# Hash attention and mixture of adapters: the last third of the attention as one group, and another order of the tail

## The chip, the core and the metric

The kernel runs on one core of one Trainium2 chip. TensorE (PE) does the matrix products, VectorE (DVE), ScalarE (ACT) and GpSimd (POOL) work beside it, and SyncE (SP) issues most of the transfers. The metric is the device time of one execution in microseconds. The profile is that of one execution; its span runs from the first to the last instruction on the core.

## The reference

There are 4 batches of 8 heads, 768 positions, head dimension 64. Each query and key gets a 6-bit bucket from the signs of its product with `proj`; a query attends to the keys of its own bucket:

```python
mask = q_bucket[:, :, :, None] == k_bucket[:, :, None, :]
scores = np.where(mask, scale * np.matmul(q, k.transpose(0, 1, 3, 2)), -1e9)
attn = np.exp(scores - np.max(scores, axis=-1, keepdims=True))
attn = attn / (np.sum(attn, axis=-1, keepdims=True) + 1e-09)
x = np.matmul(attn, v)                 # heads side by side: (B*S, H*D) = (3072, 512)
logits = x @ w_gate                    # 8 experts, the two largest are taken
w = softmax of the two logits
out = x + sum over the two experts e of w_e * ((x @ A[e]) @ B[e])   # rank 16
```

## The kernel before

**Attention.** The heads are taken in 16 pairs, four to a batch. `score` makes a tile of 1024 columns of the transposed scores in PSUM (PE, L328), and ACT turns it into weights with one exponential (L330), nine tiles for a pair. PE multiplies the weights by V, which has a column of ones for the sum (L335, and L407, L435 at the end); DVE takes the reciprocal of the sum and scales. A position index is split into 6 *slots* of 128; a slot is the unit of the second half of the kernel.

**Mixture of adapters.** It needs all 512 features of a position, so it follows a batch's last pair. For a group of slots: `xtrans` or `xtrans2` transposes the bf16 copy `xb` of x on PE and copies it to `xT`; `lgz` multiplies `xT`, in four parts of 128 features (t = 0 to 3, one for each pair of heads), by the router and the first adapter matrix side by side (`wa`) into the tile `lz` (L501); `route_a` finds the largest logits (DVE, L510, L512), `route_e` takes an exponential (ACT, L522), `route_b` makes the gate weights `gw` and the gated `zm` (DVE, L532, L534); `totals` makes the reciprocal `rt` of their sum (L545, L547); `zmtrans` transposes `zm` on PE (L555) and copies it to `zmT` (L558, DVE or ACT); `delta` multiplies by the second matrix (L571) and adds x. The addition is either one DVE instruction (L580), or, with `by_pool`, an ACT scaling (L577) and a POOL addition (L578). Each slot's output, 256 KB, then goes out by a DMA (L583).

**The end.** The order of all work is written out by hand: every engine executes its instructions in the order in which the program emits them, and a waiting instruction holds back those behind it on its engine. The last two pairs (p = 14, q = 15) are handled by `last_two` (L706), in *thirds*: third u is the slots 2u and 2u+1. Its loop runs m = 0 to 17, three steps for each of (p,0), (p,1), (q,0), (q,1), (p,2), (q,2); each step makes one score tile, and the product with V follows with `third` in three parts of eight matmuls after one matmul with `eps` that opens the tile. `third_out` writes x in float32 and has POOL cast it to `xb`; with `fast` (the thirds (q,1) and (p,2)) DVE writes `xb` itself first and x after it. The third (q,2) is different: `pieces` cuts its scores by slot into eight matmuls of 128 columns, and `sixth` handles slot 4 and then slot 5, each in its own PSUM tile with 12 matmuls; `sixth_x` writes `xb` and x, both on DVE. Below, t[0], t[1], t[2] are the groups of slots (0,1), (2,3), (4,5) of the last batch.

After the loop (L778 to L804) the program emits the rest: the second half of `sixth(4)`, the deltas of t[0], the transposes and `lgz` of t[2], then route, transposition and delta of t[1] and t[2]. The deltas of t[0] and t[1] go by ACT and POOL, those of t[2] by DVE. Outputs leave by SP's queue, but for the last ones: one and a half by ACT's queue for t[2], and slot 3 by ACT's queue as the very last instruction (L802).

**PSUM.** Eight banks: the pool `ps_s` has two tiles of two banks, `ps_v` two of one bank, `ps_t` and `ps_m` one each. A tile of a pool can be written when all readers of the tile that was there before are done, so `bank=` in a call also says whom it waits for.

Of the kernel before, what the change touches and what calls it, by code (L numbers as in the profile page):

```python
# [19 lines left out]
class Emitter:  # L20
# [266 lines left out]
    def pieces(self, p, s):  # L287
        S, out = self.S, []
        if p == self.n_pairs - 1 and s >= 6:
            for j in range(8):  # L290
                e, hk = divmod((s - 6) * 8 + j, 2 * self.T)
                h, kt = divmod(hk, self.T)
                i = 3 * e + 2
                out.append((h, kt, self.aug[p % 2][0:71, 2 * h, i * self.P:(i + 1) * self.P], 128, 128 * j))
            return out
        if p >= self.n_pairs - 2:
            for j in range(4):
                h, kt = divmod((s % 3) * 4 + j, self.T)
                q = self.aug[p % 2][0:71, 2 * h, :].rearrange("p (e c) -> p e c", e=2)
                u = s // 3  # L300
                out.append((h, kt, q[:, :, u * self.P:(u + 1) * self.P], 256, 256 * j))
            return out
        at, end = s * 1024, (s + 1) * 1024
        while at < end:
            kt, q0 = divmod(at, S)
            h, kt = divmod(kt, self.T)
            n = min(512 - at % 512, S - q0)
            out.append((h, kt, self.aug[p % 2][0:71, 2 * h, q0:q0 + n], n, at - s * 1024))
            at += n
        return out  # L310

    def p_at(self, p, h, kt, i):
        if p == self.n_pairs - 1 and i % 3 == 2:
            o = 6144 + (i // 3) * 1536 + (h * self.T + kt) * 128
        elif p >= self.n_pairs - 2:
# [98 lines left out]
    def third_out(self, p, u, fast=False):  # L414
        b, hp, sl = self.B - 1, p % self.PPB, slice(2 * u, 2 * u + 2)
        x, xb = self.x[b][:, :, hp * self.P:(hp + 1) * self.P], self.xb[b][:, hp]
        if fast:
            self.third_x(p, u, xb)
        self.third_x(p, u, x)
        if not fast:  # L420
            self.nc.gpsimd.tensor_copy(out=xb[:, sl, :], in_=x[:, sl, :])


    def sixth(self, sl, j0, j1):
        nc, P, T, D = self.nc, self.P, self.T, self.D
        p, b = self.n_pairs - 1, self.B - 1
        if j0 == 0:
            pv = self.ps_v.tile([P, 2, D + 1], F32, tag="v", name=f"pvs{sl}")
            ri = self.smallp.tile([P, 2], F32, tag="ri", name=f"ris{sl}")
            self.pvl[sl] = pv, ri  # L430
            nc.tensor.matmul(out=pv, lhsT=self.eps, rhs=self.vb[p % 3][:, :, T, :], start=True, stop=False)
        pv, ri = self.pvl[sl]
        for j in range(j0, j1):
            h, kt = divmod(j, T)
            nc.tensor.matmul(out=pv[:, h, :], lhsT=self.p_at(p, h, kt, 3 * (sl - 4) + 2),  # L435
                             rhs=self.vb[p % 3][:, h, self.slot(kt), :], start=False, stop=(j == 2 * T - 1))
        if j1 == 2 * T:
            nc.vector.reciprocal(out=ri, in_=pv[:, :, D])
            self.sixth_x(sl, self.xb[b][:, self.PPB - 1])

    def sixth_x(self, sl, dst):
        D = self.D
        pv, ri = self.pvl[sl]
        self.nc.vector.tensor_tensor(
            out=dst[:, sl, :].rearrange("p (h d) -> p h d", h=2), in0=pv[:, :, 0:D],
            in1=ri.unsqueeze(2).to_broadcast([self.P, 2, D]), op=ALU.mult)
# [43 lines left out]
    def lgz(self, b, slots, which=None, bank=None):  # L490
        nc, P = self.nc, self.P
        n = len(slots)
        if which is None or 0 in which:
# [3 lines left out]
        for i, s in enumerate(slots):  # L497
            if which is not None and i not in which:
                continue
            for t in range(self.nD):  # L500
                nc.tensor.matmul(out=lz[:, i, :], lhsT=self.xT[b][:, t, s * P:(s + 1) * P],  # L501
                                 rhs=self.wa[:, t, :], start=(t == 0), stop=(t == self.nD - 1))
# [203 lines left out]
    def last_two(self, p, q, b):  # L706
# [5 lines left out]
        for m in range(18):  # L712
# [34 lines left out]
            for at, k in ((3, 0), (6, 1), (8, 2), (11, 3), (14, 4)):  # L747
                if 0 <= m - at < 3:
                    self.third(*order[k], m - at)
                if m - at == 2:  # L750
                    self.third_out(*order[k], fast=k > 2)
# [16 lines left out]
            if m == 15:  # L768
                self.xtrans2(p, q, t[1], one)
                self.route_e(b, t[0])  # L770
                self.route_b(b, t[0])
            if m == 16:
                self.lgz(b, t[1], bank=far)
                self.route_a(b, t[1], now=False)
            if m == 17:
                self.zmtrans(b, t[0])
                self.sixth(4, 0, 8)
        self.sixth(4, 8, T2)  # L778
        self.sixth_x(4, x)
        self.route_e(b, t[1])  # L780
        self.delta(b, t[0], 0, bank=mid, by_pool=True)
        self.xtrans(p, t[2], on_act=True, bank=free)
        self.sixth(5, 0, 4)
        self.sixth(5, 4, T2)
        self.xtrans(q, (4,), on_act=True, bank=free)
        self.xtrans(q, (5,), on_act=True, bank=free)
        self.delta(b, t[0], 1, bank=mid, by_pool=True)
        self.lgz(b, t[2], (0,), bank=one)
        self.route_b(b, t[1], sums=False)
        self.lgz(b, t[2], (1,))  # L790
        self.zmtrans(b, t[1], on_act=True, bank=far)
        self.route_a(b, t[2])
        self.totals(b, t[1])
        self.delta(b, t[1], 0, by_pool=True)
        self.route_b(b, t[2], sums=False)
        self.zmtrans(b, t[2], on_act=True)
        self.sixth_x(5, x)
        self.totals(b, t[2])
        self.delta(b, t[1], 1, by_pool=True, send=False)
        self.delta(b, t[2], 0, engs=(self.nc.scalar,))  # L800
        self.delta(b, t[2], 1, engs=(self.nc.scalar, self.nc.sync))
        self.nc.scalar.dma_start(  # L802
            out=self.out[b * self.S:(b + 1) * self.S, :].rearrange("(p t) f -> p t f", t=self.T)[:, t[1][1], :],
            in_=self.acc[b, t[1]][:, 1, :])  # L804
# [47 lines left out]
```

## Time and profile before

| | |
|---|---|
| runs, median (lowest to highest of 5) | 171.21 us (170.82 to 171.58) |
| the profiled execution: its own time, its span | 173.34 us, 170.8 us |
| busy, share of the span: PE / ACT / DVE / POOL | 94% / 89% / 71% / 68% |
| granted TensorE clock, mean over the span | 0.97 |
| last exponential (L330) starts, takes | 157.32 us, 1.03 us |
| last score matmuls, last matmul of the kernel start | 156.67 us, 165.43 us |
| last output DMAs issued (SP, ACT) | 166.96 us, 167.02 us |

Times in the trace are in us from the start of the span. PE works through nearly all of it until about 157.9 us; what comes after, some 13 us, is the tail. The page's slices of 4.27 us show the granted clock at 9 tenths or more, but at 8, 5, 5 in the last three. In a merged row of the timeline the second number is from the start of the first to the end of the last instruction in it, and a matmul's end is modelled, some 0.15 us after the next one may start. A bracket behind a row gives the idle time before it and what ended it.

### The profile page before, as it was taken

How to read it: one execution, taken by the hardware profiler on the slowest of the kernel's cores; microseconds unless marked ns; L12 is line 12 of the kernel's file. 1: busy time of each engine (PE TensorE's matmuls, PEld its weight loads, DVE VectorE, ACT ScalarE, POOL GpSimd, SP SyncE). 2: the span in 40 equal slices, each digit the busy share in tenths (PEclk: the TensorE clock that was granted, in tenths of full speed). 3: DMA queues.
4: the chain of work that ended last, by engine and by line, in shares of the span. 5: the costliest groups of instructions: out<-in, count | busy, mean ns of one | idle time of the engine just before them, and what ended most of it. 6: DMA issues, size and time to landing. Idle time of an engine off the chain costs nothing.

```text
span 170.8 us, 5304 instructions
## 1 busy us (share of the span) xinstructions
PE 161.3 (94%) x2120; PEld 113.9 (67%) x2120; DVE 121.0 (71%) x327; ACT 151.9 (89%) x179; POOL 115.7 (68%) x142
## 2 busy tenths in 40 slices
PE   7999999999999999999999999999999999999660
PEld 6446667676767676767677776858676778888410
DVE  3866576565746887878687886868688785778660
ACT  3579999999999999999999999999999998998650
POOL 8289859999988668576758486776858379500370
PEclk9999999999999999999999999999999999999855
DMA  5990298999979158487577168695844050143036
GB/s 155 312 354 12 69 316 140 206 160 188 159 185 248 70 136 286 140 219 239 134 241 253 31 157 289 146 301 169 230 125 137 12 169 12 51 126 123 0 143 227
DMA packets 30546, 28.49 MB, mean 167 GB/s; under 512 B 15082, under 2 KB 28474, under 8 KB 30522
## 3 DMA queue, kind: packets, MB, share of 16 engines
q1 hardware_dynamic: 25128, 27.23, 55.5%
q0 software_dynamic: 4832, 0.27, 5.0%
q10 hardware_dynamic: 562, 0.66, 1.1%
q8 instruction: 16, 0.26, 0.7%
q14 instruction: 8, 0.07, 0.1%
HBM read 19.42 MB, written 6.29 MB: 151 GB/s over the span
## 4 chain that ended last, share of the span: by engine, by line
PE 89%; DVE 4%; ACT 1%; DMA 1%; issue 1%; DVEq 0%; SPq 0%
PE s L328 37%; PE pv L335 18%; PE tr L243 12%; PE hs L263 7%; PE dl L571 3%; PE lz L501 3%; PE hsd L147 2%; PE warm L189 1%; PE trf L126 1%; ACT P L330 1%; PE pvl L407 1%; DMA aug<-sgn 1%; DVE acc L580 1%; PE ztp L555 1%; PE xtp L484 1%
## 5 line engine op out<-in xcount | busy, mean ns | idle before, releaser
L330 ACT ACTIVATE P<-s 128x1024 bf16<-128x1024 f32 x144 | 139.9, 1026 | 6.5 <-PE s L328 4.1
L328 PE MATMUL s<-aug 71*128 71x256 bf16 (+2 forms) x420 | 86.1, 312 | 0.7 <-issue 0.4
L281 POOL CAST aug<-qkT 64x1536 bf16<-64x1536 f32 x30 | 43.9, 1462 | 7.9 <-DVE qkT L250 5.6
L335 PEld LDWEIGHTS <-P 128*128 128x128 bf16 x1008 | 42.2, 98 | 10.4
L328 PEld LDWEIGHTS <-aug 71*128 71x128 bf16 x420 | 34.1, 97 | 18.9 <-issue 10.6
L335 PE MATMUL pv<-vb,P 128*128 128x65 bf16 x1008 | 44.7, 193 | 0.0
L250 DVE TENSOR_SCALAR qkT<-tr 128x512 f32<-128x512 f32 x39 | 26.8, 686 | 9.1 <-PE tr L243 6.5
L243 PE MATMUL tr<-ident,nat 128*128 128x128 f32 x180 | 27.8, 277 | 0.0
L391 POOL CAST xb<-x 128x768 bf16<-128x768 f32 x14 | 11.5, 824 | 23.4 <-DVE x L385 20.8
L243 PEld LDWEIGHTS tr<-ident,nat 128*128 128x128 f32 x180 | 20.2, 140 | 6.9 <-DVE uni L367 2.3
L380 DVE TENSOR_TENSOR pv<-pv,uni 128x390 f32<-128x390 f32 x28 | 15.9, 568 | 2.7 <-PE pv L335 2.7
L385 DVE TENSOR_TENSOR x<-pv,ri 128x384 f32<-128x384 f32 x28 | 15.6, 557 | 1.0
L580 DVE SCALAR_TENSOR_TENSOR acc<-dl,rt,x 128x512 f32<-128x512 f32 (+1 forms) x21 | 15.0, 718 | 1.6 <-PE dl L571 1.4
L226 POOL TENSOR_TENSOR vs<-vn 128x384 f32<-128x384 f32 x16 | 15.9, 995 | 0.0
L266 DVE TENSOR_SCALAR sgn<-hs 128x384 bf16<-128x384 f32 x15 | 8.4, 558 | 10.2 <-PE hs L263 10.1
L224 POOL CAST vb<-vn 128x768 bf16<-128x768 f32 x16 | 13.2, 828 | 0.2
L263 PE MATMUL hs<-qkT,proj 128*32 128x384 f32 x120 | 12.8, 498 | 0.0
L578 POOL TENSOR_TENSOR acc<-tmp,x 128x512 f32<-128x512 f32 x4 | 5.0, 1265 | 10.7 <-ACT tmp L577 10.7
L571 PE MATMUL dl<-Bcat,zmT 128*128 128x512 bf16 x24 | 10.3, 428 | 1.9 <-DVE zmT L558 1.0
L501 PE MATMUL lz<-wa,xT 128*128 128x136 bf16 x96 | 9.6, 231 | 0.0
L367 DVE COPY uni<-un 128x130 f32<-128x130 f32 x14 | 4.1, 294 | 7.3 <-PE un L365 6.9
L229 POOL TENSOR_TENSOR vb<-vs,vs 128x128 bf16<-128x128 f32 x16 | 7.3, 457 | 1.3
(72 smaller groups left out, 136.8 us busy)
## 6 DMA issues: line engine op xcount, KB each, us to landing
vn<-in_v_dram SPq DMA_DIRECT2D x16, 384.0 KB
nat<-in_q_dram SPq DMA_DIRECT2D x15, 384.0 KB
nat<-in_k_dram SPq DMA_DIRECT2D x15, 384.0 KB
out_dram<-acc SPq DMA_DIRECT2D x7, 512.0 KB
out_dram<-acc SPq DMA_DIRECT2D x7, 256.0 KB
aug<-sgn SPq DMA_DIRECT2D x60, 9.0 KB
out_dram<-acc ACTq DMA_DIRECT2D x2, 256.0 KB
nat<-in_q_dram SPq DMA_DIRECT2D x2, 192.0 KB
```

What stands on the lines that cost most here:

```text
L226: nc.gpsimd.tensor_add(out=s3, in0=vn[:, :, 0:3, :], in1=vn[:, :, 3:6, :])
L243: nc.tensor.transpose(out=ps[:, j * P:(j + 1) * P], in_=self.nat[p][:, idx % 2, idx // 2, u * P:(u + 1) * P], identity=self.ident)
L250: nc.vector.tensor_scalar(out=out, in0=ps, scalar1=2.0 ** -5, scalar2=None, op0=ALU.mult)
L263: nc.tensor.matmul(out=ps[32 * j:32 * j + 32, :], lhsT=self.proj2, rhs=self.qkT[p][:, j * 384:(j + 1) * 384], start=True, stop=True)
L281: self.nc.gpsimd.tensor_copy(out=self.aug[p % 2][0:64, :, e * n:(e + 1) * n], in_=self.qkT[p][64 * e:64 * e + 64, :].rearrange("p (j c) -> ...
L328: nc.tensor.matmul(out=ps[:, o:o + n], lhsT=aug[0:71, 2 * h + 1, kt * P:(kt + 1) * P], rhs=q, start=True, stop=True)
L330: nc.scalar.activation(out=self.P_[p][:, s * 1024:(s + 1) * 1024], in_=ps, func=ACT.Exp, scale=128.0)
L335: self.nc.tensor.matmul(out=pv, lhsT=self.p_at(p, h, kt, i), rhs=self.vb[p % 3][:, h, self.slot(kt), :], start=(start and kt == 0), stop=( ...
L380: nc.vector.tensor_tensor(out=pv[:, 0:T, :], in0=pv[:, 0:T, :], in1=self.uni[p][:, h:h + 1, :].to_broadcast([P, T, D + 1]), op=ALU.add)
L385: nc.vector.tensor_tensor(out=self.x[b][:, :, c:c + D].rearrange("p (u e) d -> p e u d", e=2), in0=pv[:, 0:T, 0:D].rearrange("p (e u) d -> ...
L571: nc.tensor.matmul(out=ps, lhsT=self.zmT[b, slots][:, i * P:(i + 1) * P], rhs=self.Bcat, start=True, stop=True)
L580: nc.vector.scalar_tensor_tensor(out=acc[:, i, c], in0=ps[:, c], scalar=self.rt[b, slots][:, i:i + 1], in1=self.x[b][:, slots[i], c], op0= ...
```

## The change

- **Third (q,2) as one group.** `pieces` and `p_at` lose their special case: the last three score tiles are four matmuls of 256 columns, as in the other thirds. `sixth` and `sixth_x` are gone; `third(q, 2, 0..2)` makes both slots in one PSUM tile, part 0 in step 17 ahead of `zmtrans(b, t[0])`, parts 1 and 2 after the loop. `lgz` and `route_a` of t[1] move from step 16 to step 17, behind part 0 and `zmtrans`.
- **No double writes on DVE.** `third_out` has no `fast`: (q,1) and (p,2) write x alone, POOL casts. For (q,2) DVE writes `xb` only (`third_x`), and the new `third_act` lets ACT write x, in four activations of 64 columns, behind `zmT` of t[1].
- **Parts of the logits early.** `lgz` takes `ts`: t = 0 and 1 for t[2] are issued before the transposes of q, t = 2 after them, t = 3 last. Where a group's tile is made in one call, only its first matmul clears the bank and only its last ends the accumulation.
- **Order and engines.** `totals` of t[0] leaves `route_b` and comes after `route_a` of t[1]. `route_a(b, t[2])` is ahead of `zmtrans(b, t[1])`. `zmT` of t[2] is copied by DVE instead of ACT. Slot 3 (delta(t[1], 1)) is added by DVE (L580's instruction) instead of ACT and POOL, and leaves by SP's queue; slot 2 still goes by ACT and POOL, but leaves by a DMA from POOL's queue, the last instruction of the program there. The deltas of t[2] use `ps_v` (`one`), so the first waits for `third_act` to have read.

```diff
--- before.py
+++ after.py
@@ -286,13 +286,6 @@
 
     def pieces(self, p, s):
         S, out = self.S, []
-        if p == self.n_pairs - 1 and s >= 6:
-            for j in range(8):
-                e, hk = divmod((s - 6) * 8 + j, 2 * self.T)
-                h, kt = divmod(hk, self.T)
-                i = 3 * e + 2
-                out.append((h, kt, self.aug[p % 2][0:71, 2 * h, i * self.P:(i + 1) * self.P], 128, 128 * j))
-            return out
         if p >= self.n_pairs - 2:
             for j in range(4):
                 h, kt = divmod((s % 3) * 4 + j, self.T)
@@ -310,9 +303,7 @@
         return out
 
     def p_at(self, p, h, kt, i):
-        if p == self.n_pairs - 1 and i % 3 == 2:
-            o = 6144 + (i // 3) * 1536 + (h * self.T + kt) * 128
-        elif p >= self.n_pairs - 2:
+        if p >= self.n_pairs - 2:
             o = (i % 3) * 3072 + (h * self.T + kt) * 256 + (i // 3) * 128
         else:
             o = (h * self.T + kt) * self.S + i * self.P
@@ -411,39 +402,20 @@
             nc.vector.reciprocal(out=ri, in_=pv[:, :, :, D])
 
 
-    def third_out(self, p, u, fast=False):
+    def third_out(self, p, u):
         b, hp, sl = self.B - 1, p % self.PPB, slice(2 * u, 2 * u + 2)
         x, xb = self.x[b][:, :, hp * self.P:(hp + 1) * self.P], self.xb[b][:, hp]
-        if fast:
-            self.third_x(p, u, xb)
         self.third_x(p, u, x)
-        if not fast:
-            self.nc.gpsimd.tensor_copy(out=xb[:, sl, :], in_=x[:, sl, :])
-
-
-    def sixth(self, sl, j0, j1):
-        nc, P, T, D = self.nc, self.P, self.T, self.D
-        p, b = self.n_pairs - 1, self.B - 1
-        if j0 == 0:
-            pv = self.ps_v.tile([P, 2, D + 1], F32, tag="v", name=f"pvs{sl}")
-            ri = self.smallp.tile([P, 2], F32, tag="ri", name=f"ris{sl}")
-            self.pvl[sl] = pv, ri
-            nc.tensor.matmul(out=pv, lhsT=self.eps, rhs=self.vb[p % 3][:, :, T, :], start=True, stop=False)
-        pv, ri = self.pvl[sl]
-        for j in range(j0, j1):
-            h, kt = divmod(j, T)
-            nc.tensor.matmul(out=pv[:, h, :], lhsT=self.p_at(p, h, kt, 3 * (sl - 4) + 2),
-                             rhs=self.vb[p % 3][:, h, self.slot(kt), :], start=False, stop=(j == 2 * T - 1))
-        if j1 == 2 * T:
-            nc.vector.reciprocal(out=ri, in_=pv[:, :, D])
-            self.sixth_x(sl, self.xb[b][:, self.PPB - 1])
-
-    def sixth_x(self, sl, dst):
-        D = self.D
-        pv, ri = self.pvl[sl]
-        self.nc.vector.tensor_tensor(
-            out=dst[:, sl, :].rearrange("p (h d) -> p h d", h=2), in0=pv[:, :, 0:D],
-            in1=ri.unsqueeze(2).to_broadcast([self.P, 2, D]), op=ALU.mult)
+        self.nc.gpsimd.tensor_copy(out=xb[:, sl, :], in_=x[:, sl, :])
+
+
+    def third_act(self, p, u, e):
+        nc, b, D = self.nc, self.B - 1, self.D
+        pv, ri = self.pvl[p, u]
+        c = p % self.PPB * self.P
+        for h in range(2):
+            nc.scalar.activation(out=self.x[b][:, 2 * u + e, c + h * D:c + (h + 1) * D], in_=pv[:, h, e, 0:D],
+                                 func=ACT.Copy, scale=ri[:, h, e:e + 1])
 
     def third_x(self, p, u, dst):
         D = self.D
@@ -487,19 +459,20 @@
             out=self.xT[b][:, hp, t * P:(t + n) * P], in_=ps)
 
 
-    def lgz(self, b, slots, which=None, bank=None):
+    def lgz(self, b, slots, which=None, bank=None, ts=(0, 1, 2, 3)):
         nc, P = self.nc, self.P
         n = len(slots)
-        if which is None or 0 in which:
+        if (which is None or 0 in which) and 0 in ts:
             pool, tag = bank or (self.ps_m, "m")
             self.lz[b, slots] = pool.tile([P, n, self.LZ], F32, tag=tag, name=f"lz{b}_{slots[0]}")
         lz = self.lz[b, slots]
         for i, s in enumerate(slots):
             if which is not None and i not in which:
                 continue
-            for t in range(self.nD):
+            for t in ts:
                 nc.tensor.matmul(out=lz[:, i, :], lhsT=self.xT[b][:, t, s * P:(s + 1) * P],
-                                 rhs=self.wa[:, t, :], start=(t == 0), stop=(t == self.nD - 1))
+                                 rhs=self.wa[:, t, :], start=(t == 0 and (which is not None or i == 0)),
+                                 stop=(t == self.nD - 1 and (which is not None or i == n - 1)))
 
     def route_a(self, b, slots, now=True):
         nc, P, E = self.nc, self.P, self.E
@@ -748,7 +721,7 @@
                 if 0 <= m - at < 3:
                     self.third(*order[k], m - at)
                 if m - at == 2:
-                    self.third_out(*order[k], fast=k > 2)
+                    self.third_out(*order[k])
             if m == 9:
                 self.lgz(c, t[2], bank=far)
                 self.route_a(c, t[2], now=False)
@@ -768,40 +741,40 @@
             if m == 15:
                 self.xtrans2(p, q, t[1], one)
                 self.route_e(b, t[0])
-                self.route_b(b, t[0])
-            if m == 16:
+                self.route_b(b, t[0], sums=False)
+            if m == 17:
+                self.third(q, 2, 0)
+                self.zmtrans(b, t[0])
                 self.lgz(b, t[1], bank=far)
                 self.route_a(b, t[1], now=False)
-            if m == 17:
-                self.zmtrans(b, t[0])
-                self.sixth(4, 0, 8)
-        self.sixth(4, 8, T2)
-        self.sixth_x(4, x)
+        self.third(q, 2, 1)
+        self.totals(b, t[0])
         self.route_e(b, t[1])
+        self.xtrans(p, t[2], on_act=True, bank=free)
+        self.third(q, 2, 2)
+        self.third_x(q, 2, self.xb[b][:, q % self.PPB])
         self.delta(b, t[0], 0, bank=mid, by_pool=True)
-        self.xtrans(p, t[2], on_act=True, bank=free)
-        self.sixth(5, 0, 4)
-        self.sixth(5, 4, T2)
-        self.xtrans(q, (4,), on_act=True, bank=free)
-        self.xtrans(q, (5,), on_act=True, bank=free)
+        self.lgz(b, t[2], bank=one, ts=(0, 1))
+        self.xtrans(q, t[2], on_act=True, bank=free)
+        self.lgz(b, t[2], ts=(2,))
+        self.route_b(b, t[1], sums=False)
         self.delta(b, t[0], 1, bank=mid, by_pool=True)
-        self.lgz(b, t[2], (0,), bank=one)
-        self.route_b(b, t[1], sums=False)
-        self.lgz(b, t[2], (1,))
+        self.lgz(b, t[2], ts=(3,))
+        self.route_a(b, t[2])
         self.zmtrans(b, t[1], on_act=True, bank=far)
-        self.route_a(b, t[2])
         self.totals(b, t[1])
-        self.delta(b, t[1], 0, by_pool=True)
         self.route_b(b, t[2], sums=False)
-        self.zmtrans(b, t[2], on_act=True)
-        self.sixth_x(5, x)
+        self.third_act(q, 2, 0)
+        self.delta(b, t[1], 0, by_pool=True, send=False)
+        self.third_act(q, 2, 1)
+        self.zmtrans(b, t[2])
         self.totals(b, t[2])
-        self.delta(b, t[1], 1, by_pool=True, send=False)
-        self.delta(b, t[2], 0, engs=(self.nc.scalar,))
-        self.delta(b, t[2], 1, engs=(self.nc.scalar, self.nc.sync))
-        self.nc.scalar.dma_start(
-            out=self.out[b * self.S:(b + 1) * self.S, :].rearrange("(p t) f -> p t f", t=self.T)[:, t[1][1], :],
-            in_=self.acc[b, t[1]][:, 1, :])
+        self.delta(b, t[1], 1)
+        self.delta(b, t[2], 0, bank=one, engs=(self.nc.scalar,))
+        self.delta(b, t[2], 1, bank=one, engs=(self.nc.scalar, self.nc.sync))
+        self.nc.gpsimd.dma_start(
+            out=self.out[b * self.S:(b + 1) * self.S, :].rearrange("(p t) f -> p t f", t=self.T)[:, t[1][0], :],
+            in_=self.acc[b, t[1]][:, 0, :])
 
 
```

## The prediction

> **What bounds the kernel now.** I read first the page (the engines' shares and the slices of the clock), then the chain of waits that ended last, which is where a change of the end must show. From 155 us on it runs through all engines, one short step after another:
>
> ```profile
> 155.23 1.02 ACT P L330
> ...
> 157.60 0.42 DVE xb L451
> ...
> 160.13 0.30 DVE xb L444
> ...
> 161.16 0.92 PE lz L501 x8
> 162.10 0.26 DVE top L510 x2
> ...
> 163.29 0.43 DVE zm L534
> ...
> 165.28 0.75 DVE acc L580
> 166.05 0.48 DVE acc L580
> ```
>
> The columns are start and length. The tail is bound by latency: the attention of slots 4 and 5 has its `xb` at 160.42, their logits begin at 162.10, their gated `zm` at 163.29, and three DVE additions end at 166.93. Before this chain, the timeline of PE shows three places where PE stood and what released it:
>
> ```profile
> 154.37 0.38 PE L571 MATMUL dl<-Bcat,zmT 128*128 128x512 bf16 x1 [0.23 <-DVE acc L580]
> 158.97 0.39 PE L571 MATMUL dl<-Bcat,zmT 128*128 128x512 bf16 x1 [0.99 <-DVE zmT L558]
> 160.48 0.25 PE L484 MATMUL xtp<-ident_bf,xb 128*128 128x128 bf16 x1 [0.53 <-DVE xb L444]
> ```
>
> Each time DVE was late; around 157.3 to 159.3 it is busy without a break. Then the stretches of the trace (length; busy time and instructions of PE, PEld, DVE, ACT, POOL; granted clock; DMA share; GB/s):
>
> ```profile
> 143.50:146.91 3.41, 3.06 (x52) 2.32 (x50) 2.08 (x6) 2.57 (x4) 2.58 (x5) 1.00 0.07 15
> 153.74:157.15 3.41, 3.18 (x63) 2.89 (x59) 2.80 (x10) 2.78 (x4) 0.00 (x0) 1.00 0.23 94
> 157.15:160.56 3.41, 1.89 (x37) 1.39 (x35) 2.82 (x17) 2.48 (x6) 0.40 (x1) 1.00 0.15 60
> 160.56:163.97 3.41, 2.52 (x16) 1.48 (x16) 2.25 (x12) 2.04 (x5) 2.13 (x2) 0.50 0.21 79
> 161.46:162.25 0.79, 0.79 (x8) 0.55 (x5) 0.15 (x2) 0.42 (x1) 0.29 (x1) 0.50 0.00 0
> 166.25:169.30 3.05, 0.00 (x0) 0.00 (x0) 0.68 (x2) 0.00 (x0) 0.47 (x1) 0.50 0.96 344
> 169.30:170.80 1.50, 0.00 (x0) 0.00 (x0) 0.00 (x0) 0.00 (x0) 0.00 (x0) 0.50 0.00 0
> ```
>
> Two facts come out of it. PE's clock is halved from 160.56 on, after a stretch in which PE was busy for 1.89 of 3.41 us. And the end is set by transfers: four outputs of 256 KB lie back to back from 166.25 to 169.30 at 344 GB/s, 0.76 us each; the last lands at about 169.65, and 1.15 us of waits and barriers close the span at 170.8. An output needs 0.79 us from its issue (161.46) to its first byte.
>
> **The change part by part.** I follow the chain, before against after, in times of this execution.
>
> *Step 1, xb by POOL.* The xb write of (q,1) on DVE (0.42 us, at 152.90) goes; x takes its place, the addition L580 moves from 153.58 to 153.23, and PE's wait at 154.37 shrinks to 154.01. The scores of (q,2) follow 0.36 earlier, so that the exponentials, which then run back to back, start at 154.88 instead of 155.23 and end at 157.99 instead of 158.34: **-0.35**. The POOL cast (0.40, as at L421) hides: POOL has idled since 151.0, and xt needs it at 154.9. Without that cover it would cost 0.40.
>
> *Step 2, the new wait on PE.* Part 0 of third (q,2) writes the `ps_v` tile that (p,2) used, and must wait for DVE's x of (p,2). DVE: e is ready at 156.02, gw 156.05, zm 156.44, reciprocal 156.78, x 156.98 to 157.40 (steps of 0.39, 0.34, 0.20 from the rows at 156.40 to 157.60 of before; the two `totals` instructions no longer stand between). PE is done with its last score at 156.37 and stands until 157.45, **1.1 us**. Behind it on PE: zmtrans and lgz of t[1] (lgz began at 156.20 before, now at 157.91), parts 1 and 2, the transposes of p. After release: part 0 0.35, zmtrans 0.11, lgz 0.47, part 1 0.25, two transposes 0.11, part 2 0.25 (0.029 for a matmul of 65 columns, 0.055 for 128, 0.059 for 136, by their spacing before): issued by 158.99, done at 159.15. The last exponential (157.99) is in time. DVE: zmT 158.12, largest logits of t[1] 158.58, d 158.85, totals to 159.31, reciprocal 159.22, xb 159.42 to 159.84 (0.42 for 256 columns). Before it was 160.42: **-0.58**. Taking both slots after the last exponential costs nothing, since before as well the exponential was over 2 us ahead of slot 5's xb, which PE's and DVE's other work held up; if that cover were gone, part 0 and its eight matmuls (0.35) would come on top.
>
> *Step 3, early logits.* Before, PE had the transpose, a delta and all eight lgz between `xb` and the logits at 162.10 (1.68 after xb's end). After: two transposes at 159.90, done 160.18; the ACT copy 160.21 to 160.58 (0.37 for 256 columns; tmp of t[0] ends at 160.16 ahead of it); only two lgz remain behind it, at 160.62. At half clock (spacing 0.113, 0.32 to the end) they are read at 161.09: 1.25 after xb. Gain **1.01** by here. At full clock it is 160.94.
>
> *Step 4, route and transposition of t[2].* d 161.37; e on ACT behind tmp, free since 161.31: 161.56; gw 161.81, zm 162.20 to 162.62; before 163.72: **-1.10**. ztp 162.67, done 163.07; zmT on DVE (0.28) 163.11 to 163.39; totals 163.31 and 163.50. zmT of t[1] now stands behind e on ACT: 161.9 to 162.25. The four ACT writes of x are bounded by e's row above (0.21 each, 128x16; 0.27 for 128x128, I take 0.22, in two pairs); the second pair ends at about 163.4, and the first delta of t[2] needs it and zmT (163.39).
>
> *Step 5, four additions.* DVE gets slot 3: 0.75, spacing 0.66. Begins 163.58; slot 4 164.23; the halves 164.89 and 165.29 to 165.77. Before, three ended at 166.93: **-1.16**, the extra 0.66 paid by the removed wait for PE (1.09 idle before L580 at 165.28).
>
> *Step 6, the outputs.* SP issues slot 3 at 164.36, ACT slot 4 at 165.02 and half of slot 5 at 165.40, SP the other half at 165.80. On SP, slot 3 stands behind the outputs of slots 0 and 1, whose POOL additions end at 161.5 and 162.7, so nothing waits there; on ACT both issues stand behind the writes of x, over by then. POOL's addition of slot 2 (1.26) runs from 163.35 to 164.6, its DMA, the last on POOL, is issued at 164.65. At 0.79 us to the first byte, slot 3's bytes flow from 165.15 to 165.9; the remaining 768 KB from 165.85 without a gap take 2.28: the last byte at **168.1** against 169.30, **-1.2**.
>
> A POOL-issued output has no row before. The nearest are the weight loads:
>
> ```profile
> wa<-in_moe_A_dram POOLq DMA_DIRECT2D x4, 32.0 KB, 5.1
> Bcat<-in_moe_B_dram POOLq DMA_DIRECT2D x1, 128.0 KB, 4.3
> ```
>
> The last number is us from issue to landing. Bcat, with rows of 1 KB on 128 partitions, is nearest in shape, but it shared the engines with loads. [...] By the row it lands at 164.65 + 4.3 = 168.95, the span ends at 170.1, **-0.7**; by the slower row's longest (5.4), 170.05 and 171.2, **+0.4**. [...]
>
> *The clock.* [...] I take the drop at 160.56 again. [...]
>
> *Sum.* DMA-bound end 168.6 + 1.15 = 169.75 against 170.8: **-1.05** of span. The profiled execution's own time was 173.34, 2.54 more than its span and 2.13 above the median of the runs; the parts around the span don't change, so the median goes from 171.21 to about **170.15**.
>
> **The rivals.**
>
> *The gain is swallowed (170.7 to 171.7 us, middle 171.2).* POOL's DMA at 4.3 to 5.0 us from its issue would be last and eat the gain; for it, all six such DMAs of before took 3.8 to 5.4. Against it, these were many small rows, or contended. Or small waits of 0.1 us, of which I count about ten hops, add up to 1.
>
> *Slower (171.7 us): the clock falls one stretch earlier.* The new gap of 1.1 us on PE (step 2) lies across 157.15. The stretch that ends there would be busy for about 2.75 of 3.41 us (3.18, less 0.6 for the gap, with the 0.36 that moved). Nothing before says whether 80% keeps the clock: 90% did (143.50), 55% did not. If it falls there, the 1.55 us of PE work after the wait, all on the path, takes 3.1: 1.55 - 1.05 = +0.5. It decides once the drop comes before about 158.0, since then over 1.0 of it is run at half clock. The boundaries' place may differ between executions.
>
> *The change doesn't do what it says:* if slot 4's earlier start was worth more than the double writes, xb comes no earlier than 160.4; then steps 3 to 6 still give 0.5: 170.7.
>
> **How the numbers follow.** Forecast 0.62; swallowed, with the last case, 0.22; slower by the clock 0.10; slower by POOL's DMA beyond 5.0 us 0.06. About 0.3% (0.5 us) is what this measurement can tell from no change. Faster is the forecast with 0.03 of the swallowed cases, 0.65; same 0.18 of them; slower the last two and 0.01, 0.17. The forecast's own range is 169.6 to 170.7. The low end is full clock with the POOL DMA hidden: a last byte at 168.1 - 0.27, 0.35 to its landing as before, 1.15 to the end, 169.3 of span, that is -1.5 and 169.7; I put it at 169.6. The high end reaches to the slower cases, 171.6, and leaves out about half of them.
>
> **What would show it.** Right: the last exponential ends 0.35 earlier; PE waits about 1 us for DVE's x ahead of third (q,2); the logits of t[2] are read about 1 us earlier; four L580-like additions end by about 165.8; the stretch of full DMA share ends at about 168.2. Wrong: a clock that falls before 158; POOL's DMA landing last by more than 0.5 us; DVE waiting on ACT's x; the four additions apart from each other.

## The result, and the profile after

The changed kernel takes 170.31 us in the median of 25 runs (lowest 169.87), the kernel before 171.36 in 44 runs beside it; the ratio is 0.9933, 95% interval 0.9915 to 0.9951. That is 1.15 us less (0.84 to 1.45); the forecast was 1.05. The ratio is that of the executions in the usual state of the chip and leaves a few slower ones of each kernel out, so that it need not agree with the medians (1.05 us apart).

The profiled execution of the changed kernel took 169.94 us, its span is 168.2. The difference of the spans, 2.6 us, is not the change's alone: the first exponential starts at 8.98 us in the trace of before and at 8.03 here, and that offset of 0.95 stays, to within 0.02, until the tail. So I count from a point that the change doesn't move, the end of the exponential ahead of the last three: 154.60 us before, 153.63 after. From there to the end of the span it is 16.21 us before and 14.53 after, 1.68 less.

The chain that ended last, of the changed kernel (start, length, engine and line):

```profile
...
157.75 0.43 DVE xb L423
...
158.98 0.31 PE lz L473 x2
159.31 0.26 DVE top L483 x2
...
160.50 0.43 DVE zm L507
...
161.31 0.30 DVE zmT L531
...
162.46 0.74 DVE acc L553
```

It is the same kind of chain, one engine after another, only shorter: from zero, xb is done at 4.54 us (before 5.82), the logits are read at 5.68 (7.50), zm is done at 7.29 (9.12), and the timeline of DVE ends with four additions:

```profile
156.03 0.42 DVE L423 TENSOR_TENSOR x<-pvl,ril 128x256 f32<-128x256 f32 x1
...
161.79 2.19 DVE L553 SCALAR_TENSOR_TENSOR acc<-dl,rt,x 128x512 f32<-128x512 f32 x4
```

The row of PE that decides about the prediction is the one where third (q,2) opens its tile:

```profile
155.43 0.28 PE L391 MATMUL pvl<-vb,eps 128*128 128x260 bf16 x1
155.55 0.40 PE L398 MATMUL pvl<-vb,P 128*128 128x65 bf16 x8
155.96 0.29 PE L528 MATMUL ztp<-ident_bf,zm 128*128 128x128 bf16 x2
```

No bracket stands behind it, and it starts 0.6 us ahead of DVE's x at 156.03, for which it was to wait. The stretches of the changed kernel (columns as in the prediction):

```profile
154.98:158.40 3.42, 3.12 (x51) 2.50 (x49) 2.99 (x15) 3.06 (x6) 0.40 (x1) 1.00 0.38 153
158.40:161.81 3.41, 1.92 (x14) 0.72 (x12) 2.38 (x14) 2.91 (x10) 2.66 (x3) 1.00 0.21 79
...
163.30:166.45 3.15, 0.00 (x0) 0.00 (x0) 0.68 (x2) 0.00 (x0) 0.49 (x1) 0.50 0.94 333
166.45:168.20 1.75, 0.00 (x0) 0.00 (x0) 0.00 (x0) 0.00 (x0) 0.00 (x0) 0.50 0.00 0
```

The clock falls at 161.81, when nearly all of PE's work is over; before, it fell ahead of the logits. The transfers again lie back to back, for 3.15 us at 333 GB/s. And the DMA table has the row that was missing before:

```profile
out_dram<-acc POOLq DMA_DIRECT2D x1, 256.0 KB, 3.0
```

3.0 us from issue to landing, where the weight loads took 3.8 to 5.4.

### The profile page after: what moved, and what is told of

It reads as the page before. It is cut to its first block, busy times and chain, and to the rows that moved or that the text cites. A ratio compares the mean times of both kernels' runs of the same rounds, so it can differ in the third digit from the quotient of the medians.

```text
span 168.2 us, 5278 instructions
## 1 busy us (share of the span) xinstructions
PE 159.0 (95%) x2107; PEld 112.8 (67%) x2107; DVE 120.5 (72%) x323; ACT 151.3 (90%) x180; POOL 115.8 (69%) x144
## 4 chain that ended last, share of the span: by engine, by line
PE 92%; DVE 2%; DMA 1%; ACT 1%; issue 1%; DVEq 0%; SPq 0%
PE s L319 38%; PE pv L326 18%; PE tr L243 13%; PE hs L263 7%; PE lz L473 3%; PE dl L544 3%; PE pvl L398 2%; PE hsd L147 2%; PE warm L189 2%; PE trf L126 1%; DMA aug<-sgn 1%; PE ztp L528 1%; PE xtp L456 1%; DVE acc L553 1%; ACT P L321 1%
## 5 line engine op out<-in xcount | busy, mean ns | idle before, releaser
L319 PE MATMUL s<-aug 71*128 71x256 bf16 (+1 forms) x408 | 86.1, 316 | 0.7 <-issue 0.4
L319 PEld LDWEIGHTS <-aug 71*128 71x128 bf16 x408 | 33.6, 97 | 18.7 <-issue 10.2
L553 DVE SCALAR_TENSOR_TENSOR acc<-dl,rt,x 128x512 f32<-128x512 f32 (+1 forms) x22 | 15.5, 718 | 0.3 <-PE dl L544 0.3
L544 PE MATMUL dl<-Bcat,zmT 128*128 128x512 bf16 x24 | 9.3, 393 | 1.2 <-ACT zmT L531 1.0
L228 POOL TENSOR_TENSOR vs<-vs 128x128 f32<-128x128 f32 x16 | 7.3, 456 | 1.3
```

What stands on the lines that cost most here:

```text
L319: nc.tensor.matmul(out=ps[:, o:o + n], lhsT=aug[0:71, 2 * h + 1, kt * P:(kt + 1) * P], rhs=q, start=True, stop=True)
L553: nc.vector.scalar_tensor_tensor(out=acc[:, i, c], in0=ps[:, c], scalar=self.rt[b, slots][:, i:i + 1], in1=self.x[b][:, slots[i], c], op0= ...
```

## The experiments

The theory to test: the tail is a chain of short steps, and each step that is taken off it shows at the end of the span. Two rivals: most of the difference between the traces is the place where the clock fells PE to half speed (*clock rival*); or the transfers set the end and the chain doesn't matter (*transfer rival*). The times of runs scatter by about 1 us, and at least a part of that lies ahead of the tail (the first exponential starts between 7.95 and 9.09 us in these traces), so each run is read twice: by its ratio, and by the length of its tail from the zero above to the end of the span. The tails of the changed kernel's two traces agree to 0.01 us.

| run | ratio to before (95%) | tail, us | clock falls, us from zero |
|---|---|---|---|
| before, first trace | 1 | 16.21 | 6.0 |
| before, second trace | | 15.46 | 8.6 |
| before, one line moved | 0.9976 (0.9958 to 0.9994) | 14.78 | 10.9 |
| before, idle matmuls | 0.9980 (0.9962 to 0.9998) | 15.22 | 10.5 |
| changed | 0.9933 (0.9915 to 0.9951) | 14.53 | 8.2 |
| changed, once more | 0.9942 (0.9916 to 0.9968) | 14.53 | 7.7 |
| with the wait | 0.9973 (0.9955 to 0.9992) | 15.30 | 8.4 |
| late logits | 0.9945 (0.9922 to 0.9968) | 14.72 | 9.1 |
| idle matmuls | 0.9938 (0.9911 to 0.9964) | 14.55 | 11.4 |
| DVE writes xb | 0.9969 (0.9947 to 0.9991) | 14.82 | 8.4 |
| DVE writes x of (q,2) | 0.9949 (0.9925 to 0.9972) | 14.51 | 9.2 |
| slot 3 by ACT and POOL | 0.9945 (0.9923 to 0.9966) | 14.81 | 7.8 |
| slot 2 sent by SP | 0.9929 (0.9904 to 0.9954) | 14.26 | 7.7 |
| slot 2 early, by SP | 0.9914 (0.9889 to 0.9940) | 14.13 | 9.0 |

**The changed kernel once more**, to see what repeats.

> The changed kernel once more, as the measure for the three runs beside it. Both theories: 1.0 to 1.3 us below the kernel before. In its trace the latency theory expects the same marks as in the first one, counted from the last exponential but two: first matmul of third (q,2) without a wait, xb ready 4.3 us after that exponential starts. Where the clock falls may move by up to a stretch of 3.4 us; if the clock rival is right, the tail's length moves with it by over 0.5 us.

Ratio 0.9942; every mark of the tail within 0.01 us of the first trace, though the clock fell 0.46 earlier. xb is ready 4.25 after the start of that exponential, as expected.

**The wait that the prediction counted.**

```diff
             if m == 17:
+                hold = self.ps_v.tile([self.P, 2], F32, tag="v", name="hold")
+                self.nc.tensor.matmul(out=hold, lhsT=self.eps, rhs=self.eps[:, 0:2], start=True, stop=True)
                 self.third(q, 2, 0)
+                self.nc.tensor.matmul(out=hold, lhsT=self.eps, rhs=self.eps[:, 0:2], start=True, stop=True)
```

`hold` keeps the tile that third (q,2) had, so that it gets the other one.

> The changed kernel, but third (q,2) gets the other tile of ps_v, the one that DVE reads for x of (p,2); so the wait that the prediction counted (step 2) is there. Latency theory: part 0 starts 1.05 us later than in the changed kernel, xb comes 0.7 us later, and the kernel takes 0.5 to 0.8 us more than the changed one, some 0.4 below the kernel before. Rival (the end is set by the clock and the output transfers, xb is not what the tail waits for): under 0.2 us more.

PE's timeline of this run:

```profile
155.43 0.17 PE L747 MATMUL hold<-eps 128*128 128x2 bf16 x1
156.50 0.29 PE L391 MATMUL pvl<-vb,eps 128*128 128x260 bf16 x1 [0.91 <-DVE x L423]
```

Now the bracket is there, with x as its releaser. The matmul starts 1.07 us later than without the wait, xb comes 0.77 later, and the tail is 0.77 longer; the ratio rises from 0.9942 to 0.9973, 0.53 us. Shown: the 0.77 us by which the wait holds xb back go to the end of the span one for one, past the transfers. The transfer rival expected under 0.2. This run is also the kernel as the prediction pictured it, and it is only 0.46 us faster than before (0.14 to 0.77).

**Step 3 undone: all logits of t[2] together.**

```diff
-        self.lgz(b, t[2], bank=one, ts=(0, 1))
         self.xtrans(q, t[2], on_act=True, bank=free)
-        self.lgz(b, t[2], ts=(2,))
...
-        self.lgz(b, t[2], ts=(3,))
+        self.lgz(b, t[2], bank=one)
```

> The changed kernel with all eight logit matmuls of t[2] issued together, behind the copies of both transposes (step 3 undone). Latency theory: six more matmuls behind the copy, 6 x 0.059 = 0.35 us at full clock, 6 x 0.113 = 0.68 at half; the kernel takes 0.35 to 0.7 us more than the changed one. Rival (transfers set the end): under 0.2 us more.

The tail is 0.19 us longer, and the ratio (0.9945) cannot tell it from the changed kernel. The latency theory missed (it expected 0.35 to 0.7); the rival's number is met, but not for its reason, since the run with the wait shows that the chain does set the end. PE's timeline tells why it is so little:

```profile
159.00 0.28 PE L456 MATMUL xtp<-ident_bf,xb 128*128 128x128 bf16 x2 [0.52 <-DVE xb L423]
159.26 0.38 PE L544 MATMUL dl<-Bcat,zmT 128*128 128x512 bf16 x1
159.47 0.75 PE L473 MATMUL lz<-wa,xT 128*128 128x136 bf16 x8
```

Slot 4's four matmuls come first among the eight, and only the fourth reads the part of xT that is being copied: three run while ACT still copies, to 159.70. So five stand behind the copy instead of two, and three of 0.059 us (the spacing that the expectation counts with) are 0.18.

**PE kept busy: idle matmuls in its gap.**

```diff
-        self.delta(b, t[1], 0, by_pool=True, send=False)
+        self.delta(b, t[1], 0, by_pool=True, send=False, idle=4)
...
-        self.delta(b, t[2], 0, bank=one, engs=(self.nc.scalar,))
+        self.delta(b, t[2], 0, bank=one, engs=(self.nc.scalar,), idle=1)
```

with `idle` matmuls of `eps` and `Bcat` into the tile ahead of the delta's own.

> The changed kernel with four idle matmuls of 512 columns (0.86 us in all) in PE's gap of 1.15 us before the delta of slot 2, and one before the first delta of t[2]; they write into the tile that the delta overwrites. Latency theory: little rests on the clock behind that gap, 0.0 to 0.3 us less or 0.2 more. Clock rival: the clock does not fall before the last matmul, and the kernel takes 0.4 us or more less than the changed one.

The clock now holds past the last matmul (11.4 us from zero), and the tail is the same, 14.55 against 14.53, with xb, the logits, zm and the last addition where they were to 0.01 us. So the idle matmuls held nothing up, and in the changed kernel the clock costs nothing.

**Step 1 undone: DVE writes xb of (q,1) and (p,2).**

```diff
+        if fast:
+            self.third_x(p, u, xb)
         self.third_x(p, u, x)
-        self.nc.gpsimd.tensor_copy(out=xb[:, sl, :], in_=x[:, sl, :])
+        if not fast:
+            self.nc.gpsimd.tensor_copy(out=xb[:, sl, :], in_=x[:, sl, :])
```

> The changed kernel with DVE again writing xb itself, ahead of x, for (q,1) and (p,2) (step 1 undone). Latency theory: the last three exponentials begin 0.35 us later, and the second write pushes DVE back by 0.33 just before it reads the logits of t[1] and third (q,2): xb 0.3 later still. 0.4 to 0.7 us more than the changed kernel. Rival (double writes on DVE were hidden, the gain is elsewhere): under 0.2 more.

ACT and PE of this run:

```profile
156.33 1.02 ACT L321 ACTIVATE P<-s 128x1024 bf16<-128x1024 f32 x1 [0.62 <-PE s L319]
```

```profile
155.48 0.38 PE L547 MATMUL dl<-Bcat,zmT 128*128 128x512 bf16 x1 [0.23 <-DVE acc L556]
```

In the changed kernel the gap ahead of that exponential is 0.29, here 0.62 as in the kernel before: 0.33 us, by the wait for the addition that the prediction named. The second push, of (p,2), doesn't show: the tail is 0.29 longer in all, under the 0.4 that was the least expected. The ratio agrees (0.9969 against 0.9933 and 0.9942, 0.5 to 0.6 us, with an interval that holds 0.3).

**DVE instead of ACT writes x of (q,2).**

```diff
-        self.third_act(q, 2, 0)
...
-        self.third_act(q, 2, 1)
+        self.third_x(q, 2, x)
```

> The changed kernel with x of third (q,2) written by DVE in one instruction of 0.42 us behind zm of t[2], in place of the four ACT writes. DVE idles 0.38 us there in the changed kernel. Latency theory: under 0.15 us more, or a little less since the first delta of t[2] no longer waits for ACT. Rival (moving the f32 writes to ACT is itself worth something): 0.3 us or more.

Tail 14.51. Nothing, as the latency theory expected: the 0.42 us fall into DVE's idle 0.38 ahead of zmT. Moving these writes to ACT is worth nothing here.

**Steps 5 and 6 undone: slot 3 by ACT and POOL.**

```diff
-        self.delta(b, t[1], 0, by_pool=True, send=False)
+        self.delta(b, t[1], 0, by_pool=True)
...
-        self.zmtrans(b, t[2])
+        self.zmtrans(b, t[2], on_act=True)
...
-        self.delta(b, t[1], 1)
+        self.delta(b, t[1], 1, by_pool=True, send=False)
...
-        self.nc.gpsimd.dma_start(
-            out=self.out[b * self.S:(b + 1) * self.S, :].rearrange("(p t) f -> p t f", t=self.T)[:, t[1][0], :],
-            in_=self.acc[b, t[1]][:, 0, :])
+        self.nc.scalar.dma_start(
+            out=self.out[b * self.S:(b + 1) * self.S, :].rearrange("(p t) f -> p t f", t=self.T)[:, t[1][1], :],
+            in_=self.acc[b, t[1]][:, 1, :])
```

> The changed kernel with slot 3 added by ACT and POOL again, zmT of t[2] copied by ACT, slot 2 sent by SP and slot 3 by ACT as the last instruction (step 5 and 6 undone). Latency theory: ACT reaches zmT 0.6 us later behind tmp and the writes of x, POOL's second addition ends at 10.4 us from the start of the last exponential but two, and the last byte comes 0.3 to 0.5 us later than in the changed kernel. Rival (transfers alone set the end, it does not matter who adds): under 0.15 more.

Tail 14.81, 0.28 longer. DVE in this run:

```profile
162.99 1.54 DVE L553 SCALAR_TENSOR_TENSOR acc<-dl,rt,x 128x512 f32<-128x512 f32 x3 [1.78 <-PE dl L544]
```

DVE stands 1.78 us until the first delta of t[2], while ACT works through scalings and writes of x; with the change it fills that time with slot 3. In the ratio (0.9945) it is not to be told from nothing. This run also takes slot 2 off POOL's queue, and the next run shows that this alone shortens the tail by 0.27. Against that run, where slot 2 goes by SP as well, adding slot 3 on ACT and POOL makes the tail 0.55 longer (14.81 against 14.26).

**Slot 2 sent by SP instead of POOL.**

```diff
         self.delta(b, t[1], 1)
+        self.nc.sync.dma_start(
+            out=self.out[b * self.S:(b + 1) * self.S, :].rearrange("(p t) f -> p t f", t=self.T)[:, t[1][0], :],
+            in_=self.acc[b, t[1]][:, 0, :])
         self.delta(b, t[2], 0, bank=one, engs=(self.nc.scalar,))
         self.delta(b, t[2], 1, bank=one, engs=(self.nc.scalar, self.nc.sync))
-        self.nc.gpsimd.dma_start(
-            out=self.out[b * self.S:(b + 1) * self.S, :].rearrange("(p t) f -> p t f", t=self.T)[:, t[1][0], :],
-            in_=self.acc[b, t[1]][:, 0, :])
```

> The changed kernel with slot 2's output issued by SP, behind slot 3's, in place of POOL. The transfers lie back to back for 3.05 us from slot 3's first byte on, whoever issues: 0.15 us less to 0.15 more than the changed kernel. Rival (POOL's transfer is late and holds the end, as the prediction feared): 0.3 us or more less than the changed kernel.

```profile
163.20:166.35 3.15, 0.00 (x0) 0.00 (x0) 0.70 (x2) 0.00 (x0) 0.00 (x0) 0.50 0.93 333
166.35:167.80 1.45, 0.00 (x0) 0.00 (x0) 0.00 (x0) 0.00 (x0) 0.00 (x0) 0.50 0.00 0
```

The bytes take the same 3.15 us at the same 333 GB/s. But the tail is 0.27 shorter, more than the 0.15 that the latency theory allowed and nearly what the rival asked: what follows the last byte is 1.45 us here and 1.75 with POOL's transfer. In the changed kernel the landing of POOL's transfer is not the last one (166.24 us, against 166.95 for slot 5's half), so it doesn't hold the end as the prediction feared; the end comes later all the same. The last landing follows the last byte by 0.55 us with POOL's transfer, and by 0.35 in the first trace of before, where no output goes by POOL; why is not known, since no run takes it apart. The ratios (0.9929 against 0.9942) are too close to show 0.27 us by themselves.

**The kernel before once more.**

> The kernel before once more, for a second trace of it. Latency theory: its tail, counted from the start of the last exponential but two, has the same order and the same waits (PE for zmT 1.0 us, for xb 0.5), and ends 15.1 to 15.6 us later, wherever the clock falls. Clock rival: with the clock falling a stretch later than in the first trace, it ends at 14.7 or below, and most of the difference to the changed kernel is gone.

PE in this second trace:

```profile
158.50 0.39 PE L571 MATMUL dl<-Bcat,zmT 128*128 128x512 bf16 x1 [1.00 <-DVE zmT L558]
...
160.02 0.23 PE L484 MATMUL xtp<-ident_bf,xb 128*128 128x128 bf16 x1 [0.53 <-DVE xb L444]
160.30 0.64 PE L501 MATMUL lz<-wa,xT 128*128 128x136 bf16 x8
...
162.65 0.39 PE L555 MATMUL ztp<-ident_bf,zm 128*128 128x128 bf16 x2 [0.74 <-DVE zm L534]
162.83 1.28 PE L571 MATMUL dl<-Bcat,zmT 128*128 128x512 bf16 x2
```

The logits in the first trace:

```profile
160.95 1.11 PE L501 MATMUL lz<-wa,xT 128*128 128x136 bf16 x8
```

The waits are the same, but the clock falls at 162.68, and the eight logit matmuls take 0.64 us instead of 1.11. The logits are read 1.01 us after xb is done instead of 1.68, and the tail is 15.46, 0.75 shorter than in the first trace of the same kernel. From the start of the last exponential but two it is 14.83: between the two expectations. So the clock rival is right about at least 0.75 of the 1.68 us between the first two traces. What is left, 0.93, is not yet the change alone: in this trace too the transposes of zm and the deltas behind them run at half clock, as the last two rows of the second trace show. The run of before with idle matmuls, below, takes that out.

**One line moved in the kernel before.**

```diff
-        self.delta(b, t[0], 0, bank=mid, by_pool=True)
         self.xtrans(p, t[2], on_act=True, bank=free)
         self.sixth(5, 0, 4)
         self.sixth(5, 4, T2)
+        self.delta(b, t[0], 0, bank=mid, by_pool=True)
```

> The kernel before with one line moved: the first delta of t[0] stands behind the second half of the attention of slot 5 instead of ahead of it. Latency theory: what held xb up in the kernel before was PE waiting 1.0 us for zmT of t[0] with slot 5's matmuls queued behind it; xb comes 0.4 to 0.6 us earlier, and the kernel takes 0.3 to 0.6 us less than before. Rival (taking both slots as one group, or the removed double writes, made xb earlier): under 0.15 us less.

```profile
162.38 0.53 PE L435 MATMUL pvs<-vb,P 128*128 128x65 bf16 x12
162.87 0.39 PE L571 MATMUL dl<-Bcat,zmT 128*128 128x512 bf16 x1
...
163.87 0.23 PE L484 MATMUL xtp<-ident_bf,xb 128*128 128x128 bf16 x1 [0.37 <-DVE xb L444]
```

PE's wait of 1.0 us is gone, xb comes 0.51 us earlier and the tail is 14.78. (This execution took 176.24 us, against a median of 171.11; in it the clock was at half for 6.8 us ahead of the tail, and only its tail is used.) The tail is 0.68 shorter than the second trace, but here the clock held to 10.9 us from zero; against the run with idle matmuls, where it held as well, it is 0.44 shorter, of the 0.69 of the whole change. By the ratio it is 0.4 us, 0.1 to 0.7, of 1.15. What helps is that slot 5's attention no longer stands behind a delta that waits; that both slots are one group is not needed for it.

**PE kept busy in the kernel before**, with matmuls into tiles that are overwritten.

```diff
             self.pvl[sl] = pv, ri
+            for _ in range(8 if sl == 4 else 0):
+                nc.tensor.matmul(out=pv, lhsT=self.eps, rhs=self.vb[p % 3][:, :, T, :], start=True, stop=True)
...
+        for _ in range(6):
+            self.nc.tensor.matmul(out=self.lz[b, t[2]][:, 0, :], lhsT=self.eps, rhs=self.wa[:, 0, :], start=True, stop=True)
         self.xtrans(q, (5,), on_act=True, bank=free)
```

> The kernel before with 8 idle matmuls of 130 columns ahead of slot 4's product with V and 6 of 136 columns in PE's wait for slot 5's xb, 0.8 us in all, in tiles that are overwritten. Clock rival: the clock stays up through the logits of t[2], and the kernel takes 0.4 us or more less than before. Latency theory: 0.3 less to 0.3 more.

The clock holds to 10.5 us from zero, past the last matmul; tail 15.22, 0.24 shorter than the second trace and 0.99 shorter than the first. xb is done at 5.83, the logits are read at 6.84 and zm is done at 8.46, as in the second trace, so the idle matmuls held nothing up; only what stands behind zm is faster. With the clock out of play on both sides, then, the change shortens the tail by 0.69 us (15.22 to 14.53), and the clock rival is right about 0.99 of the 1.68. The ratio, 0.9980, is a gain of 0.34 us (0.03 to 0.65) against the mixture of executions of before, between the 0.3 of the one theory and the 0.4 of the other.

**A further version.** From the changed kernel, with the DMA of POOL's queue taken out as well, so that slot 2 leaves by SP ahead of slot 3:

```diff
-        self.route_a(b, t[2])
+        self.route_a(b, t[2], now=False)
         self.zmtrans(b, t[1], on_act=True, bank=far)
+        self.route_e(b, t[2])
...
-        self.third_act(q, 2, 0)
-        self.delta(b, t[1], 0, by_pool=True, send=False)
+        self.delta(b, t[1], 0, by_pool=True)
+        self.third_act(q, 2, 0)
         self.third_act(q, 2, 1)
```

> The changed kernel with slot 2 sent by SP ahead of slot 3, the exponential of t[2] behind the copy of zmT of t[1] on ACT, and the writes of x behind slot 2's scaling. Latency theory: ACT idles 0.27 us before that exponential, so the copy is free; slot 2 is ready 0.5 us earlier; the transfers, which lie back to back, begin 0.2 us earlier and end 0.2 earlier than with slot 2 on SP alone, 0.4 to 0.6 us before the changed kernel's. Rival (the last additions hold the end, not the transfers): no more than 0.1 earlier than with slot 2 on SP alone.

Ratio 0.9914 (0.9889 to 0.9940), 1.5 us below before; tail 14.13, 0.13 shorter than with slot 2 on SP alone and 0.40 shorter than the changed kernel. That lies between the two expectations (0.2, and at most 0.1), and by the ratio alone this version cannot be told from the changed kernel, whose interval overlaps. POOL's addition ends 0.49 earlier and DVE's additions where they did, so the last 0.13 comes from the transfers beginning earlier.

## Why the prediction was right, point by point

The number was right by luck, since two errors cancel: a wait was counted that is not there (*Step 2*), and the sum was taken from an execution of before whose clock fell unusually early (*The sum*). With the wait put in, the change is worth 0.46 us. From zero, in us:

| mark | before, first / second trace / idle matmuls | predicted | changed | with the wait |
|---|---|---|---|---|
| third (q,2) opens its tile | | 2.85 | 1.80 | 2.87 |
| xb of slots 4 and 5 done | 5.82 / 5.83 / 5.83 | 5.24 | 4.54 | 5.31 |
| logits of t[2] read | 7.50 / 6.84 / 6.84 | 6.49 | 5.68 | 6.45 |
| zm of t[2] done | 9.12 / 8.46 / 8.46 | 8.02 | 7.29 | 8.07 |
| last addition done | 12.33 / 11.67 / 11.23 | 11.17 | 10.35 | 11.12 |
| end of the span | 16.21 / 15.46 / 15.22 | 15.15 | 14.53 | 15.30 |

- *Step 1* was right: the exponentials start 0.29 after zero instead of 0.63, and undoing it costs 0.29 at the end. Not seen: with the logits of t[1] no longer ahead of the last score, the last two exponentials close up (0.90 between their starts instead of 1.06), another 0.16.
- *Step 2* failed. "Part 0 of third (q,2) writes the `ps_v` tile that (p,2) used, and must wait for DVE's x of (p,2)." It got the other tile, that of the transposes of t[1], whose copy stands earlier in the program than x of (p,2) and was over at 154.82. I had counted the two tiles in turn. That the pool gives the one whose readers end first in the order of the program fits this case and is not tested beyond it. The trace of before already spoke against turns: there slot 4's tile is the next after the same two, and PE opened it without a wait, 0.55 us ahead of DVE's x of (p,2):

```profile
157.39 0.22 PE L431 MATMUL pvs<-vb,eps 128*128 128x130 bf16 x1
157.94 0.41 DVE L451 TENSOR_TENSOR x<-pvl,ril 128x256 f32<-128x256 f32 x1
```

The working of the step itself holds: the run that restores the wait follows the predicted column to within 0.1 us down to the last addition. The wait was 0.77 us of the end.
- *Step 3* was right in the hop and wrong in what it was compared with. From xb to the logits 1.25 us was expected and 1.14 measured, the difference being the clock. But the 1.68 of the kernel before held 0.67 of half clock, as its second trace shows (1.01). Against that, early logits gain nothing; undoing them costs 0.19.
- *Steps 4 and 5* were right: from the logits to zm 1.61 (expected 1.53), from there to the end of the additions 3.06 (3.15); undoing the move of slot 3 costs 0.28, or 0.55 where slot 2 goes by SP in both.
- *Step 6*: POOL's transfer was mis-sized, 3.95 us to its landing (the 168.6 of the forecast) against 3.0 measured. No run shows that 168.6: issued at 163.20, the transfer had its first packet at 164.84, 1.64 us later, and landed at 166.24, 0.71 ahead of the last landing. The rows of the loads, 4.3 and at most 5.4 us to the landing, did not hold for it either: it hid in the other transfers. It still costs 0.27 in what follows the last byte, which the forecast does not have. The stretch of full transfers, 3.05 us expected from slot 3's first byte, is 3.15. Behind the last addition the forecast has 3.98 us to the end of the span, and 4.18 were measured, with the wait as without it.
- *The clock* was taken to fall at 160.56 again, 5.96 from zero; it fell at 8.2, and the run with idle matmuls shows that nothing hangs on it after the change. The rival of a fall one stretch earlier did not come about: without the wait the stretch that it feared for was busy for 3.12 of 3.42 us. Even with the wait the stretch was busy for 2.50 of 3.41 us (0.73) and the clock held. Nor does a run show the 0.27 us that the low end of the range takes off for a full clock: with idle matmuls the clock held past the last matmul and the tail stayed at 14.55 against 14.53.
- *The sum.* The forecast took 1.06 off the tail. Against the first trace the change takes 1.68: 0.77 more for the missing wait, with 0.15 lost elsewhere. But 0.99 of that trace's tail was an early fall of the clock, as the run of before with idle matmuls shows, and the change alone takes 0.69. The first trace was also a rare one: its mean granted clock was 0.970, and of the 154 executions of before that were timed beside the experiments 4 have 0.970, 33 have 0.979 to 0.984 (the second trace has 0.980), and 117 have 0.985 or more (the run with idle matmuls has 0.986). Another small part lies outside the span, which the forecast took as unchanged: an execution's time exceeds its span by 1.93 us in the median of those 154 and by 1.77 in the median of the changed kernel's 25; the cause of that is open. By an estimate the falls of the clock add 0.08 on the average (0.99 us in 4 of 154 and 0.24 in 33 of 154). These parts, 0.69, 0.16 and 0.08, come to 0.93, which lies within the interval of the measured 1.15 (0.84 to 1.45); whether the rest is more than noise is open.

## What to carry to other kernels

In a chain of short steps look first for a waiting instruction at the head of an in-order queue: one line that took a delta from ahead of the last attention gave 0.44 of the 0.69 us that the whole reordering takes off the tail. Before a wait on a PSUM tile is priced, find out which tile of the pool the program gets, since it may not be the one that turns would give; a trace in which the same tiles follow each other can show it. And where the clock falls within the stretch that one studies, a second trace of the same kernel is worth more than any argument: the base of this sum moved by 0.75 us between two of them, and the mean clocks of the other executions tell which of them is the rare one.

## What was not expected of the hardware

In the first traces of both kernels and in the second trace of before, the granted clock fell from 1.00 to 0.50 within the tail: at 160.56 us after a stretch in which PE's matmuls were busy for 1.89 of 3.41 us (0.55), in the changed kernel at 161.81 after 1.92 of 3.41 us (0.56), and in the second trace of before at 162.68 after 1.62 of 3.42 us (0.47). It had held after the stretch ahead of that one, with 3.18 of 3.41 us (0.93), 3.12 of 3.42 us (0.91) and 2.41 of 3.41 us (0.71). No gap of PE in the stretch ahead of the fall was over 1.01 us (0.99 before, 1.01 after). Nor does the longest gap set the stretches apart: in the second trace of before the clock held after the stretch with the gap of 1.00 us (at 158.50) and fell after the next one, whose longest was 0.74 (at 162.65). In these three traces it is the busy share that separates them; what sets the clock is not shown by them.

These are the stretches of that trace (0.71, 0.47, and half clock from there):

```profile
155.85:159.26 3.41, 2.41 (x49) 2.02 (x46) 2.95 (x15) 2.52 (x5) 0.00 (x0) 1.00 0.38 154
159.26:162.68 3.42, 1.62 (x20) 0.95 (x18) 2.69 (x14) 2.87 (x8) 2.53 (x2) 1.00 0.21 79
162.68:166.09 3.41, 1.98 (x5) 0.33 (x5) 1.98 (x6) 1.06 (x2) 2.53 (x2) 0.50 0.50 186
```
